# Tails on alternate partitions, a later load of q's first tail, and two batches' features dealt anew, in an attention kernel with a feed-forward layer

## The chip, the cores and the metric

One core of one Trainium2 chip. The metric is the device time of one launch in microseconds (us). A run that is over 1.5% above the fastest of its kernel is called slow, and ratios use the others, the fast ones.

## The reference

Eight batches of eight heads with 576 positions of 64 elements; linear attention with a cosine weight, then a feed-forward layer with a squared ReLU.

```python
def phi(x, c, s):                       # c, s: cos and sin of pi/2 * position / 576
    r = np.maximum(x, 0.0)
    return np.concatenate([r * c, r * s], axis=-1)
q_p, k_p = phi(q, cos_w, sin_w), phi(k, cos_w, sin_w)
kv  = np.einsum('bhsf,bhsd->bhfd', k_p, v)
z   = np.sum(k_p, axis=2)
num = np.einsum('bhsf,bhfd->bhsd', q_p, kv)
den = np.einsum('bhsf,bhf->bhs', q_p, z)[..., None] + 1e-06
x   = (num / den) ...                   # to (4608, 512): positions by heads*64
r   = np.maximum(x @ w_in, 0.0)         # 512 -> 2048
out = (r * r) @ w_out                   # 2048 -> 512
```

## The kernel before

A batch has 576 positions: four tiles of 128 ("main", 1 MB for each of q, k and v) and a tail of 64. The tails of the upper and the lower four heads share one tile: heads 0 to 3 on partitions 0 to 63, heads 4 to 7 on 64 to 127.

```python
def load(src, nm, b, eng):
    main = inp.tile([P, H, J, D], F32, name=nm, tag=nm, bufs=2)
    tail = inp.tile([P, HH, D], F32, name=nm + "t", tag=nm + "t", bufs=2)
    eng.dma_start(out=main[:, :, :, :], in_=...)
    for g in range(2):
        eng.dma_start(
            out=tail[g * TAIL : (g + 1) * TAIL, :, :],
            in_=src[b, g * HH : (g + 1) * HH, MAIN:S, :].rearrange("h p d -> p h d"),
        )
```

TensorE's work is a list of 144 slots (`gemm1` and `gemm2` of all batches). Attention's small pieces are hung on slots by hand: `k` are the slots in which k and v of a batch get their features, `f` those of q, `kv` the product, `d` the division. `qpT` is q's features transposed by DMA, `xT` the attention output transposed by DMA; both, and most loads, are issued by SP, in order. w_in, w_out and the loads of batches 1 to 3 are issued by GpSimd.

```python
at(14, load_batch, 3, nc.gpsimd, "qkv")
plan(2, k=(21, 22, 23, 24, 25), f=(18, 19, 20, 22, 23), kv=(26, 26), d=(27, 28, 29, 31, 33))
plan(3, k=(30, 32, 33, 34, 35), f=(27, 29, 31, 32, 33), kv=(36, 36), d=(37, 38, 39, 40, 41))
for b in range(4, B):
    at(second[b - 3] + 6, load_batch, b, nc.sync, "kv")     # slot 32 for batch 4
    at(first[b - 2] + 9, load_batch, b, nc.sync, "q")       # slot 43 for batch 4
    ...
```

One more tile matters for what follows, though the argument of the change does not mention it: a table of zeros for TensorE's warm-up, `zeros = const.tile([P, FP], BF16)`, 1024 bytes in each partition. It stands ahead of all weights and inputs in SBUF.

## Time and profile before

| | before |
|---|---|
| time, median of 4 runs | 293.31 us (292.41 to 293.62) |
| span of the profiled run | 291.0 us |
| TensorE (PE) busy | 281.0 us, 97% |
| PE idle 19 to 64 us | 0.20 us |
| PE idle 64 to 110 us | 1.17 + 0.61 + 1.31 us |
| PE idle 110 to 250 us | 0.09 + 0.29 us |

A windows view gives, for a stretch of the span, how long each engine was busy; the stretch less PE's busy time is PE's idle time. Columns: stretch, length, busy us of PE, PEld, DVE, ACT and POOL, the granted clock, the DMA engines' busy share, GB/s.

```profile
19.00:64.00 45.00, 44.80 (x491) 34.29 (x489) 29.95 (x72) 26.16 (x38) 19.66 (x28) 1.00 1.01 281
```

DMA is full here (share 1.01), and TensorE waits for nothing.

### The profile page before, as it was taken

To read this page: it belongs to the slowest core of one execution; us is meant where nothing else is said; L and a number is where in the kernel's file an instruction comes from. 1 tells how busy PE (TensorE), PEld (TensorE's weight loads), DVE (VectorE), ACT (ScalarE), POOL (GpSimd) and SP (SyncE) were. 2 spreads that over 40 slices of the span, in tenths; PEclk is the share of its full clock that TensorE was granted. 3 is DMA by queue.
4 is the path that set the end of the run, shared out by engine and by line. 5 is a ranking of instruction groups with operands and counts; after the bars stand their busy time and mean duration, and the time that the engine had idled before them with its cause. 6 is when DMAs were issued, how large, how long until landed. Compare 5 with 4: busy or idle time off the path is not lost.

```text
span 291.0 us, 7292 instructions
## 1 busy us (share of the span) xinstructions
PE 281.0 (97%) x3045; PEld 236.1 (81%) x3045; DVE 201.5 (69%) x450; ACT 164.7 (57%) x251; POOL 39.2 (13%) x67
## 2 busy tenths in 40 slices
PE   8999999998999989999999999999999999999994
PEld 3479855888677979898988888988998888889883
DVE  1467665596399487877588777977677877546584
ACT  3565752779748749655783358835695451265110
POOL 1552505750000000000002000000000000000011
PEclk9999999999999999999999999999999999999999
DMA  6999994999649996799519995399809540300014
GB/s 218 299 206 286 356 227 150 352 363 285 103 120 163 291 203 177 176 289 262 167 73 196 314 206 164 92 254 297 221 16 214 131 48 2 144 2 2 0 76 142
DMA packets 76641, 53.04 MB, mean 182 GB/s; under 512 B 52000, under 2 KB 71712, under 8 KB 76608
## 3 DMA queue, kind: packets, MB, share of 16 engines
q1 hardware_dynamic: 66816, 29.24, 43.7%
q0 software_dynamic: 9648, 23.20, 27.1%
q8 instruction: 24, 0.39, 0.5%
q10 hardware_dynamic: 144, 0.13, 0.1%
q14 instruction: 9, 0.07, 0.1%
HBM read 36.70 MB, written 9.44 MB: 159 GB/s over the span
## 4 chain that ended last, share of the span: by engine, by line
PE 83%; DVE 5%; DMA 4%; ACT 3%; SPq 2%; issue 1%; DVEq 0%
PE hps L383 40%; PE ya L525 9%; PE yc L525 8%; PE yu L525 7%; PE yv L525 5%; PE num L310 3%; DMA q<-in_q_dram 3%; PE kz L241 3%; PE yps L432 2%; PE yh L432 2%; PE yps L456 2%; DMA qpT<-qpt 2%; DVE ysb L537 2%; ACT rt L391 1%; PE tq L284 1%; SPq L69 1%
## 5 line engine op out<-in xcount | busy, mean ns | idle before, releaser
L383 PEld LDWEIGHTS <-w1sb 128*128 128x128 bf16 x1312 | 112.9, 98 | 13.6 <-issue 2.9
L383 PE MATMUL hps<-xT,w1sb 128*128 128x256 bf16 (+1 forms) x1056 | 119.0, 269 | 1.1 <-DVE ysb L537 0.6
L391 ACT ACTIVATE rt<-hps 128x1024 bf16<-128x1024 f32 x72 | 73.7, 1024 | 66.7 <-PE hps L383 43.3
L398 DVE TENSOR_TENSOR gT<-rt 128x1024 bf16<-128x1024 bf16 x64 | 43.9, 686 | 21.4 <-ACT rt L391 21.3
L525 PEld LDWEIGHTS <-gs 128*128 128x128 bf16 x480 | 46.9, 98 | 5.5
L525 PEld LDWEIGHTS <-gT 128*128 128x128 bf16 x312 | 29.8, 98 | 3.5
L410 POOL DMA_DIRECT2D out_dram<-ysb x14 | 7.7, 549 | 173.0 <-DVE ysb L537 145.6
L181 ACT ACTIVATE kp<-k,sin_col 128x512 bf16<-128x512 f32 x32 | 22.4, 718 | 3.1 <-DMA k<-in_k_dram 3.1
L324 DVE TENSOR_TENSOR x<-num,rden 128x512 bf16<-128x512 f32 x32 | 22.1, 691 | 1.1
L181 ACT ACTIVATE qp<-q,sin_col 128x512 bf16<-128x512 f32 x32 | 22.1, 722 | 1.2 <-DMA q<-in_q_dram 1.2
L320 DVE TENSOR_SCALAR den<-num 128x8 f32<-128x8 f32 (+1 forms) x40 | 6.5, 163 | 21.2 <-PE num L310 21.2
L521 DVE TENSOR_TENSOR gs<-gT 128x1024 bf16<-128x1024 bf16 x26 | 17.8, 683 | 0.0
L383 PE MATMUL hps<-xTt,w1sb 128*128 128x128 bf16 x256 | 15.1, 219 | 0.8 <-ACT rt L391 0.8
L171 DVE TENSOR_SCALAR qp<-q,cos_col 128x512 bf16<-128x512 f32 x32 | 14.7, 485 | 1.7 <-DMA q<-in_q_dram 1.7
L525 PE MATMUL yc<-w2sb,gs 128*128 128x256 bf16 x120 | 15.6, 273 | 0.0
L525 PE MATMUL ya<-w2t,gs 128*128 128x256 bf16 x120 | 15.6, 273 | 0.0
L525 PE MATMUL yu<-w2sb,gs 128*128 128x256 bf16 x120 | 15.6, 273 | 0.0
L525 PE MATMUL yu<-w2t,gs 128*128 128x256 bf16 x120 | 15.6, 273 | 0.0
L576 ACT COPY s<-yu 128x256 f32<-128x256 f32 x15 | 5.6, 373 | 16.6 <-PE yu L525 16.6
L200 ACT CAST vext<-v 128x512 bf16<-128x512 f32 x23 | 14.2, 615 | 1.3 <-DMA v<-in_v_dram 1.3
L525 PE MATMUL yc<-w2sb,gT 128*128 128x256 bf16 x104 | 13.5, 273 | 0.0
L525 PE MATMUL ya<-w2sb,gT 128*128 128x256 bf16 x104 | 13.5, 273 | 0.0
(93 smaller groups left out, 333.0 us busy)
## 6 DMA issues: line engine op xcount, KB each, us to landing
out_dram<-ysb POOLq DMA_DIRECT2D x14, 512.0 KB, 4.5
k<-in_k_dram SPq DMA_DIRECT2D x5, 1024.0 KB, 7.7
v<-in_v_dram SPq DMA_DIRECT2D x5, 1024.0 KB, 9.0
q<-in_q_dram SPq DMA_DIRECT2D x5, 1024.0 KB, 5.6
q<-in_q_dram POOLq DMA_DIRECT2D x3, 1024.0 KB, 12.4
k<-in_k_dram POOLq DMA_DIRECT2D x3, 1024.0 KB, 10.1
v<-in_v_dram POOLq DMA_DIRECT2D x3, 1024.0 KB, 8.8
w1sb<-in_moe_w_in_dram POOLq DMA_DIRECT2D x4, 512.0 KB, 8.6
```

The costliest lines, as they stand in the source:

```text
L171: nc.vector.tensor_scalar(out=dst[:, :, 0:D], in0=src, scalar1=0.0, scalar2=cos_col[:, j : j + 1], op0=ALU.max, op1=ALU.mult,)
L181: nc.scalar.activation(out=dst[:, :, D:F], in_=src, func=ACTF.Relu, scale=sin_col[:, j : j + 1])
L200: copy(out=vx[:, j, h0:h1, 0:D], in_=piece("v", b, j)[:, h0:h1, :])
L241: nc.tensor.matmul(out=kz[:, half, hh * E1 : (hh + 1) * E1], lhsT=lhsT, rhs=rhs, start=(j == 0 and hh == 0), stop=(j == J and hh == HH - 1),)
L310: nc.tensor.matmul(out=out, lhsT=lhsT, rhs=kvz[:, half * HH + hh, :], start=True, stop=True)
L324: nc.vector.tensor_tensor(out=x_of(b, j).rearrange("p (b k) (l d) -> p b k l d", b=n, l=2), in0=n4[:, :, :, 0:D].rearrange("p b (k l) d -> ...
L383: nc.tensor.matmul(out=out, lhsT=w1sb[:, kb, hb * P : (hb + 1) * P], rhs=rhs, start=(kb == 0), stop=(kb == KB - 1),)
L391: nc.scalar.activation(out=rt[:, :, :], in_=hps[:, :, :], func=ACTF.Relu)
L398: nc.vector.tensor_tensor(out=dst, in0=rt[:, :, :], in1=rt[:, :, :], op=ALU.mult)
L432: nc.tensor.matmul(out=ypss[b][tt], lhsT=gTs[b][:, hb, tt * P : (tt + 1) * P], rhs=w2sb[:, hb, :], start=(hb == 0), stop=(hb == HB - 1),)
L521: nc.vector.tensor_tensor(out=t[:, :, :], in0=in0, in1=in1, op=op)
L525: nc.tensor.matmul(out=acc, lhsT=lhs[:, hb, :], rhs=rhs[:, hb, :], start=(hb == 0), stop=(hb == HB2 - 1),)
```

## The change

The intent: let the tail loads reach all ports of SBUF and save four matmuls for each batch; get w_in 0.13 MB earlier; and move features of batches 2 and 3 between ScalarE and VectorE, so that the waits between 64 and 110 us go. The core of the diff:

```diff
-    def load(src, nm, b, eng):
-        main = inp.tile([P, H, J, D], F32, name=nm, tag=nm, bufs=2)
-        tail = inp.tile([P, HH, D], F32, name=nm + "t", tag=nm + "t", bufs=2)
 ...
+            kqv[nm, b] = inp.tile([P, NB * D], F32, name=nm, tag=nm, bufs=2)
 ...
+                out=tail_of(nm, b).rearrange("(p g) h d -> p g h d", g=2)[:, g],
 ...
-    zeros = const.tile([P, FP], BF16, name="zeros")
+    zeros = const.tile([P, P], BF16, name="zeros")
 ...
+    half_of = const.tile([P, 2], F32, name="half_of")
 ...
+            for g in range(2):
+                dst, half = vextts[b % 2][:, g, :, 0:D], half_of[:, g : g + 1]
+                if eng is nc.scalar:
+                    eng.activation(out=dst, in_=piece("v", b, j), func=ACTF.Copy, scale=half)
 ...
-            at(k[j], att_k, b, j, feat_cos_act if shared and j % 2 else feat_cos)
-            at(k[j], att_v, b, j, nc.scalar if shared and (b > 2 or j % 2) else nc.vector)
+            at(k[j], att_k, b, j, feat_cos_act if j in act_cos else feat_cos)
+            at(k[j], att_v, b, j, nc.scalar if j in act_v else nc.vector)
 ...
         d=(27, 28, 29, 31, 33),
+        act_cos=(),
+        act_v=(1,),
 ...
-        k=(30, 32, 33, 34, 35),
-        f=(27, 29, 31, 32, 33),
-        kv=(36, 36),
-        d=(37, 38, 39, 40, 41),
+        k=(27, 28, 30, 31, 32),
+        f=(33, 34, 35, 36, 36),
+        kv=(37, 37),
+        d=(38, 39, 40, 41, 42),
+        act_cos=(0, 1, 2, 3),
 ...
-        at(second[b - 3] + 6, load_batch, b, nc.sync, "kv")
+        at(36 if b == 4 else second[b - 3] + 6, load_batch, b, nc.sync, "kv")
 ...
-        load_batch(0, nc.sync, "kvq")
+        load_batch(0, nc.sync, "kv")
+        load_main("q", 0, nc.sync)
 ...
+        load_tail("q", 0, nc.gpsimd)
```

Main and tail now share one tile. With heads of both halves on alternate partitions, one matmul over all 128 partitions serves two heads: v's tail is copied twice, once with the odd and once with the even partitions set to zero (`half_of`). Batch 2 gives ScalarE's cosines and one v copy to VectorE; batch 3 has k first and q later, its cosines on ScalarE; the load of batch 4 moves from slot 32 to 36.

## The prediction

> **What bounds the kernel now.** I read the page first: the busy shares and the chain that ended last.
>
> ```profile
> PE 281.0 (97%) x3045; PEld 236.1 (81%) x3045; DVE 201.5 (69%) x450; ACT 164.7 (57%) x251; POOL 39.2 (13%) x67
> ...
> PE 83%; DVE 5%; DMA 4%; ACT 3%; SPq 2%; issue 1%; DVEq 0%
> ```
>
> TensorE is the bound: 281.0 of 291.0 us busy. The change removes almost no TensorE work, so it can win only the 10 us in which TensorE stands. The stretches (columns: span, then busy us of PE, PEld, DVE, ACT, POOL, the clock, DMA share, GB/s) say where those are:
>
> ```profile
> 0.00:19.00 19.00, 16.94 (x134) 8.48 (x135) 8.45 (x27) 10.14 (x18) 8.68 (x19) 1.00 0.97 247
> ...
> 64.00:78.00 14.00, 12.83 (x167) 10.70 (x166) 7.86 (x17) 13.34 (x20) 0.18 (x1) 1.00 1.04 239
> 78.00:96.00 18.00, 17.39 (x172) 13.53 (x171) 14.27 (x36) 12.17 (x21) 1.06 (x2) 1.00 0.65 142
> 96.00:110.00 14.00, 12.69 (x173) 11.23 (x170) 10.83 (x25) 7.72 (x12) 0.00 (x0) 1.00 1.10 228
> 110.00:130.00 20.00, 19.91 (x229) 17.80 (x227) 15.88 (x38) 13.97 (x25) 1.06 (x2) 1.00 0.80 212
> 130.00:250.00 120.00, 119.71 (x1335) 107.21 (x1334) 90.60 (x196) 68.81 (x105) 5.89 (x11) 1.00 0.67 168
> ```
>
> From 110 to 250 us only 0.4 us are idle: what is gained before 110 us reaches the end undiminished, and later batches can only lose. Between 64 and 110 us 1.17 + 0.61 + 1.31 = 3.1 us are idle; that is where batches 2 and 3 have their features. Before 19 us the matmuls are mostly warm-up, so "busy" there hides a wait for loads. The rest of the idle time, about 4 us, is the last additions and the last store, which the change leaves alone.
>
> The timeline names the three idle places. In 64 to 78 us ScalarE is busy 13.34 of 14 us:
>
> ```profile
> 71.02 1.01 ACT L391 ACTIVATE rt<-hps 128x1024 bf16<-128x1024 f32 x1
> 71.93 0.71 ACT L181 ACTIVATE kp<-k,sin_col 128x512 bf16<-128x512 f32 x1
> 72.06 0.69 DVE L398 TENSOR_TENSOR gT<-rt 128x1024 bf16<-128x1024 bf16 x1 [1.57 <-ACT rt L391]
> 72.08 1.95 PE L383 MATMUL hps<-xTt,w1sb 128*128 128x128 bf16 x32 [0.84 <-ACT rt L391]
> ...
> 77.05 0.30 PE L241 MATMUL kz<-vextt,kpt 64*128 64x65 bf16 x8 [0.33 <-ACT kpt L181]
> ```
>
> Features of batch 2 stand ahead of `rt` in ScalarE's queue, so the PSUM buffer comes free late (0.84 us), and the tail of k is late (0.33 us). At 90.59 us the next batch's first matmul waits 0.61 us for VectorE. The third place:
>
> ```profile
> 96.88 0.55 SPq L64 DMA_DIRECT2D v<-in_v_dram  x1
> 97.53 3.61 SPq L69 DMA_DIRECT2D vt<-in_v_dram  x2
> 101.23 2.07 SPq L342 DMA_TRANSPOSE xTt<-xt  x1
> 103.41 1.20 SPq L267 DMA_TRANSPOSE qpT<-qpt  x1
> 108.38 0.32 PE L310 MATMUL num<-kvz,qpT 128*64 128x65 bf16 x8 [1.31 <-DMA qpT<-qpt]
> ```
>
> The SP queue is in order. The loads of batch 4 (93.36 to 101.14 us) hold up the transpose of batch 3's q tail, and TensorE waits 1.31 us for it.
>
> **What the skill says.** (1) "SBUF — State Buffer", section "Door 1: The DMA port swizzle", says that partitions 0 to 63 reach only 8 of the 16 ports (196 against 328 GB/s at 1 MiB). This is what alternate partitions aim at. The trace agrees only in part: from 5.5 to 6 us, when 432 of 468 packets are the tail of k, the mean is 279 GB/s, against 314 GB/s for 1 KB packets from 2.5 to 5 us. Two tail halves in flight seem to use both groups of ports already. (2) "DMA: Bandwidth & Descriptors", section "Issuing engines are not separate DMA queues", says that loads from all queues interleave on the same 16 engines. So q's tail, moved to the GpSimd queue, is not carried for nothing; it only comes later. (3) "TensorE: Matmul & The Clock Gate", section "Back-to-back issue gap", makes time follow the moving columns, not the contraction rows. The trace agrees: eight 256-column matmuls are 0.87 us on the chain, 109 ns each.
>
> **The change part by part.**
>
> *Start.* The first real matmul is at 18.74 us and hangs on q, which lands at 13.6 us behind k, v and two tails in the same queue. Both tails together are 1024 packets over 16 engines, 64 each. At the 279 GB/s above, 0.26 MB take 0.94 us; at 314 GB/s 0.84 us; at best, estimated as a third less per packet, 0.6 us. So q lands 0.1 to 0.35 us earlier. q's own tail stood behind q, so taking it away gains q nothing; it frees 0.13 MB, about 0.4 us, for w_in, whose slices reach TensorE just in time. Against this: the v tail is now two VectorE operations (the old one 0.28 to 0.41 us, the new ones estimated at the 0.34 us of the k tail's, so +0.3 us) and the copy of kz is two (0.59 becomes 2 x 0.37, the 256-column copies' duration). kvz was ready at 13.02 us and its reader starts at 15.85 us, so both fit. I take **-0.3 us**.
>
> *Tail matmuls.* Eight of 65 columns at 30 ns (40 in 1.21 us) become four of 130 at 55 ns: 0.24 to 0.22 us per batch, **-0.1 us** in all. The tail of `num` now loads every second column as weights; I expect no cost.
>
> *Batch 2 re-dealt.* ScalarE loses two cos (0.62 us of pitch each) and one v copy (0.51), 1.75 us; VectorE gains 2 x 0.48 + 0.42 + 0.3 = 1.7 us and has 6.1 idle in 64 to 78. Walking ScalarE from `rt` at 67.74 with those pitches, the `rt` that freed the buffer at 72.04 is done at 71.3, and the k tail at 75.4, before its matmuls. TensorE's full 1.17 us come back, less 0.25 for the buffer freed at 71.3 instead of 71.05: **-0.9 us**.
>
> *Batch 3 re-dealt.* Its k moves ahead (slots 27 to 32, cos all on ScalarE), its q behind (33 to 36). VectorE loses 5 operations before 90 us, so the 0.61 us wait should fall to the 0.27 us seen at other batch ends: **-0.35 us**. ScalarE then has 4 x (0.62 + 0.61 + 0.51) + 0.41 + 0.8 + four copies, 10 us, in some 11.5: tight, but it fits. The k/v load of batch 4 moves from slot 32 to 36, behind the q tail transpose, which removes its wait: **-1.3 us**.
>
> Together 0.3 + 0.1 + 0.9 + 0.35 + 1.3 = 2.95 us less, if nothing replaces these waits.
>
> **Rivals.** *A: the later load of batch 4 is itself too late.* Slot 36 ends near 94 us in the changed kernel. ScalarE's `rt` and two q features follow, so the second transpose is issued near 95.8 and the load near 98 to 99, 5 us later than the old 93.36. Old: first transpose issue at 91.67, v landed at 106.4, 14.7 us later. New: 95.8 + 14 = about 109.5 to 110. Slot 42, whose first ScalarE work includes v, would be reached at 105, so v's copy wants its data at 107. From the first v copy (old 110.61) to the end of the v tail (116.81) are 6.2 us, plus 0.45 for the second masked copy. So the kz tail starts near 109.5 + 6.65 = 116.1 instead of 117.57. The net gain of all parts up to there is then 1.5 us, not 2.95: a DMA wait of some 1.5 us takes the place of those removed. Time about 291.8. For it: all issue times come from one in-order queue. Against it: the five-us shift is a walk, and every 1 us of error moves the result by 1.
>
> *B: the second masked v copy on ScalarE holds up every later batch.* Per batch +0.4 (v tail) +0.15 (kz copy). Between the old v tail's end and its matmuls are 0.76, 0.83 and 0.82 us in batches 4, 5 and 6, so it fits. If I am wrong by 0.5 us in four batches it costs 2 us: time 292 to 293.
>
> *C: nothing hides.* All waits go and the load is in time: 293.25 - 2.95 = 290.3; a start quicker by another 0.9 us through the ports makes 289.4.
>
> **Range and chances.** A at 291.8 gets 55%, C at 290.3 gets 35%, B at 292.7 gets 10%: the weighted mean is 291.4 us. The low end is C with the quicker start, the high end A with half of B's loss. Over 2% faster would be under 287.4 us and needs more than all the idle time before 270 us that I found, so 4%; over 2% slower needs a new wait of 9 us, so 1%.
>
> **What would show it.** `rt` no longer holds TensorE near 72 us, and the first batch-3 matmul waits 0.3 us or less. No wait for qpT near 107 us. q lands between 13.2 and 13.5 us and `hps` starts near 18.4. Near 105 to 117 us ScalarE waits 2 to 4 us for v of batch 4 (A) or not (C). From 120 to 250 us TensorE is idle under 0.5 us; if it is idle for more at every kz tail, B is right. Wrong would be: 256-byte packets much quicker with q landing before 13 us, or a wait for w_in, w_out or batch 1's loads between 20 and 45 us, since two more small loads stand ahead of them in the GpSimd queue.

## The result and the profile after

The changed kernel took **296.22 us** (median of 4 runs, 295.61 to 297.04) against 293.31 us. The ratio of the fast runs is 1.0106, with a 95% interval of 1.007 to 1.0142. Ratios here are the mean time of one kernel's fast runs over that of the other's of the same rounds, so not quite the ratio of the medians that are quoted. The change is slower by 1%, and outside the predicted range. The page of the changed kernel, its busy line and its chain by engine:

```profile
PE 281.4 (95%) x3008; PEld 236.0 (80%) x3013; DVE 203.5 (69%) x461; ACT 167.5 (57%) x263; POOL 39.8 (14%) x68
...
PE 70%; DMA 20%; DVE 5%; POOL 2%; issue 1%; SPq 1%; DVEq 0%; ACT 0%
```

PE's work is the same (281.4 us), but it stands for 13.4 us instead of 10.0, and the share of DMA in the chain that ended last rose from 4% to 20%. The windows view of the changed kernel tells where:

```profile
0.00:19.00 19.00, 16.44 (x120) 8.22 (x121) 8.41 (x33) 9.80 (x18) 7.83 (x18) 1.00 0.92 231
19.00:64.00 45.00, 43.73 (x474) 33.15 (x474) 29.34 (x70) 25.05 (x38) 17.66 (x25) 1.00 0.97 249
64.00:78.00 14.00, 13.72 (x179) 11.95 (x175) 11.12 (x26) 12.68 (x19) 3.64 (x6) 1.00 1.07 311
78.00:96.00 18.00, 17.37 (x166) 12.99 (x165) 13.10 (x32) 13.89 (x25) 1.06 (x2) 1.00 0.60 134
96.00:110.00 14.00, 13.84 (x180) 12.16 (x177) 10.66 (x24) 9.43 (x14) 0.00 (x0) 1.00 0.96 208
110.00:130.00 20.00, 16.22 (x182) 14.06 (x176) 13.54 (x33) 11.77 (x23) 1.06 (x2) 1.00 1.03 215
130.00:250.00 120.00, 119.67 (x1335) 107.29 (x1334) 91.14 (x199) 72.14 (x112) 5.36 (x10) 1.00 0.75 173
```

PE's idle time, before and after: 2.06 to 2.56 (0 to 19 us), 0.20 to 1.27, 1.17 to 0.28, 0.61 to 0.63, 1.31 to 0.16, 0.09 to **3.78** (110 to 130 us), 0.29 to 0.33. The re-deal did what it was to do at 64 to 78 and 96 to 110 us (2.0 us gained). Two new losses are larger: 3.7 us at 110 to 130 us and 1.1 us at 19 to 64 us.

The one at 19 to 64 us, from the chain that ended last (start, us, what):

```profile
30.89 10.95 DMA w2sb<-in_moe_w_out_dram
41.88 0.59 PE yh L497 x2
```

The second quarter of w_out needs 10.95 us from issue to landing, and the first product that reads this quarter waits for it, 0.91 us. The one after 110 us, from the timeline (start, us, engine, line, operation; in brackets the idle time before it and what ended it):

```profile
95.01 6.71 SPq L321 DMA_TRANSPOSE qpT<-qp  x2
...
105.34 0.47 SPq L84 DMA_DIRECT2D v<-in_v_dram  x1
...
112.93 0.62 ACT L244 CAST vext<-v 128x512 bf16<-128x512 f32 x1 [3.15 <-DMA v<-in_v_dram]
...
115.20 0.36 ACT L641 COPY s<-yu 128x256 f32<-128x256 f32 x1
115.22 0.53 SPq L84 DMA_DIRECT2D q<-in_q_dram  x1
115.61 1.03 PE L590 MATMUL yu<-w2sb,gs 128*128 128x256 bf16 x8 [1.91 <-ACT s L641]
...
121.16 1.33 ACT L220 ACTIVATE qp<-q,sin_col 128x512 bf16<-128x512 f32 x2 [1.26 <-DMA q<-in_q_dram]
...
122.52 5.86 SPq L321 DMA_TRANSPOSE qpT<-qp  x2
...
127.91 0.42 PE L364 MATMUL num<-kvz,qpT 128*128 128x65 bf16 x8 [1.44 <-DMA qpT<-qp]
```

Batch 4's v is loaded only behind batch 3's transposes and lands at 112.9 us. ScalarE stands 3.15 us before v's copy; the copy `s` that frees a PSUM buffer of the running product stands behind it in ScalarE's queue, so TensorE loses 1.91 us in a product that has nothing to do with batch 4. Then q of batch 4, issued behind further transposes at 115.22 us, is late as well and costs another 1.44 us. That is rival A of the prediction, but more than twice as large as it was worked out: 3.7 us more idle time, against 1.5.

### The profile page after: what moved, and what is told of

The parts are those of the page before. It is cut to its first block, busy times and chain, and to the rows that moved or that the text cites. A ratio compares the mean times of both kernels' runs of the same rounds, so it can differ in the third digit from the quotient of the medians.

```text
span 294.8 us, 7240 instructions
## 1 busy us (share of the span) xinstructions
PE 281.4 (95%) x3008; PEld 236.0 (80%) x3013; DVE 203.5 (69%) x461; ACT 167.5 (57%) x263; POOL 39.8 (14%) x68
## 4 chain that ended last, share of the span: by engine, by line
PE 70%; DMA 20%; DVE 5%; POOL 2%; issue 1%; SPq 1%; DVEq 0%; ACT 0%
PE hps L448 33%; PE yc L590 8%; PE ya L590 8%; DMA qpT<-qp 7%; PE yu L590 7%; DMA q<-in_q_dram 6%; PE yv L590 4%; DMA w2sb<-in_moe_w_out_dram 4%; PE num L364 3%; DMA v<-in_v_dram 3%; PE yh L497 2%; PE yps L497 2%; PE kz L284 2%; DVE ysb L602 1%; PE yps L521 1%; POOL w1sb L147 1%
## 5 line engine op out<-in xcount | busy, mean ns | idle before, releaser
L448 PEld LDWEIGHTS <-w1sb 128*128 128x128 bf16 x1312 | 112.9, 98 | 12.4 <-issue 1.7
L220 ACT ACTIVATE kp<-k,sin_col 128x512 bf16<-128x512 f32 (+1 forms) x40 | 26.2, 675 | 3.5 <-DMA k<-in_k_dram 3.5
L244 ACT CAST vext<-v 128x512 bf16<-128x512 f32 x22 | 13.5, 614 | 4.7 <-DMA v<-in_v_dram 4.7
L210 DVE TENSOR_SCALAR kp<-k,cos_col 128x512 bf16<-128x512 f32 (+1 forms) x28 | 12.0, 441 | 4.9 <-DMA k<-in_k_dram 4.9
L364 PEld LDWEIGHTS <-qpT 128*128 128x128 bf16 (+1 forms) x240 | 10.0, 100 | 5.8 <-DMA qpT<-qp 3.1
L364 PE MATMUL num<-kvz,qpT 128*128 128x65 bf16 (+1 forms) x240 | 11.7, 195 | 2.2 <-DMA qpT<-qp 2.0
```

What stands on the lines that cost most here:

```text
L210: nc.vector.tensor_scalar(out=dst[:, :, 0:D], in0=src, scalar1=0.0, scalar2=cos_col[:, c : c + 1], op0=ALU.max, op1=ALU.mult,)
L220: nc.scalar.activation(out=dst[:, :, D:F], in_=src, func=ACTF.Relu, scale=sin_col[:, c : c + 1])
L244: copy(out=vext_of(b, j)[:, h0:h1, 0:D], in_=piece("v", b, j)[:, h0:h1, :])
L364: nc.tensor.matmul(out=out, lhsT=lhsT, rhs=kvz[:, half * HH + hh, :], start=True, stop=True)
L448: nc.tensor.matmul(out=out, lhsT=w1sb[:, kb, hb * P : (hb + 1) * P], rhs=rhs, start=(kb == 0), stop=(kb == KB - 1),)
```

## The experiments

Each was run in five rounds against the kernel before on the same chip, after a profiled run. The ratios leave slow runs out: one run of six in e1, e2, e4, e8, e14 and e16, more where the text says so.

### First call: one part undone, or alone

**e1_load_at_32**: the changed kernel with batch 4's k and v at slot 32.

```diff
-        at(36 if b == 4 else second[b - 3] + 6, load_batch, b, nc.sync, "kv")
+        at(second[b - 3] + 6, load_batch, b, nc.sync, "kv")
```

> The changed kernel with one thing undone: k and v of batch 4 are loaded at slot 32 again, not 36. Theory L (the later load is the largest loss): of the 3.78 us in which TensorE stands between 110 and 130 us, under 0.6 are left; in exchange the transpose of batch 3's q tail stands behind the loads again, and 0.8 to 1.3 us of waiting for qpT come back between 96 and 110 us. Net about 2.4 us less: 293.8 us (293.0 to 294.6). Rival M (the masked v copies and slower transposes of the new layout make batch 4 late, not the slot): time stays within 1 us of 296.2 and at least 2 us of idle time stay between 110 and 130 us.

Measured: **302.25 us**, ratio 1.0298 (1.026 to 1.0335). Both theories missed. From the timeline:

```profile
97.97 7.76 SPq L321 DMA_TRANSPOSE qpT<-qp  x2
...
105.70 0.54 PE L364 MATMUL num<-kvz,qpT 128*128 128x65 bf16 x8 [5.22 <-DMA qpT<-qp]
106.05 3.47 PE L448 MATMUL hps<-xT,w1sb 128*128 128x256 bf16 x16
109.36 0.41 PE L364 MATMUL num<-kvz,qpT 128*128 128x65 bf16 x8
```

With the re-deal, q of batch 3 gets its features after k, so not only its tail but both of its large transposes stand behind the loads; TensorE waits 5.22 us. It then pays a second time: 16 matmuls of 256 columns take 3.47 us instead of the 1.91 us that they take elsewhere in this trace, at a granted clock of 0.88 for the stretch from 96 to 110 us. The Trainium skill ("TensorE: Matmul & The Clock Gate", section "HAM oscillation — how this bites in real kernels") warns of idle gaps over about 3.4 us; this trace agrees, with 5.22 us. (In e7, below, a wait of 1.92 us preceded the same fall.) So the later load is not an oversight of the change: the re-deal needs it.

**e2_qtail_first**: the changed kernel with q of batch 0 loaded whole by SP.

```diff
-        load_batch(0, nc.sync, "kv")
-        load_main("q", 0, nc.sync)
+        load_batch(0, nc.sync, "kvq")
 ...
-        load_tail("q", 0, nc.gpsimd)
```

> The changed kernel with q of batch 0 loaded whole on SP again, no load of its tail in the GpSimd queue. Theory Q (the two small loads push the first quarter of w_out behind further loads): the wait of the first yh for w2sb near 41 us disappears, TensorE idle between 19 and 64 us falls from 1.27 to 0.2 to 0.4 us, the first quarter of w_out is issued near 16.5 us again instead of 20.3; time about 295.2 us (294.8 to 295.6). Rival (the wait comes from slower packets in the run, whatever the order): the wait stays at 0.6 us or more and the time within 0.4 us of 296.2.

Measured: 296.46 us, ratio 1.0089 (1.0055 to 1.0123), like the changed kernel. The wait for w2sb fell only from 0.91 to 0.58 us. Theory Q falls for the most part: the order of the two small loads is not what makes w_out late.

**e3_deal_only**: the kernel before with the re-deal and the load at slot 36, nothing of the layout.

```diff
+        act_cos=(), act_v=(1,),                        # plan of batch 2
-        k=(30, 32, 33, 34, 35), f=(27, 29, 31, 32, 33), kv=(36, 36), d=(37, 38, 39, 40, 41),
+        k=(27, 28, 30, 31, 32), f=(33, 34, 35, 36, 36), kv=(37, 37), d=(38, 39, 40, 41, 42),
+        act_cos=(0, 1, 2, 3),                          # plan of batch 3
-        at(second[b - 3] + 6, load_batch, b, nc.sync, "kv")
+        at(36 if b == 4 else second[b - 3] + 6, load_batch, b, nc.sync, "kv")
```

> The kernel before with the re-deal of batches 2 and 3 and the load at slot 36 alone; tails on two halves, q loaded whole first. Theory L: the re-deal gains its 2.0 us before 110 us, the late load loses 3 to 3.7 us after it: 294.6 us (294.0 to 295.2), TensorE idle in 110 to 130 us 3 to 3.8 us. Rival M (layout makes batch 4 late): idle there under 1 us and a time of about 291.3 us.

Measured: 292.67 us, ratio 0.9988 (0.9943 to 1.0032): no loss and no proven gain. In the profiled run, its slowest, PE stood 2.93 us between 110 and 130 us. So the late load costs there as theory L says, though less than in the changed kernel (3.78 us), and the whole is 1.9 us under L's number. That points to something in the layout that is dear.

**e4_layout_only**: the changed kernel with everything undone but the layout: the edits of e1 and e2 together, and the diff of e3's two plans the other way round.

> The changed kernel with everything undone but the alternate partitions (with the masked v copies, the four tail matmuls, the merged buffers, the split copy of kz). Theory N (the layout itself does nothing): 293.3 us, within 0.4 of before; 256-byte packets take 18 ns; k, v and q land within 0.3 us of before. Rival P (ports): q lands 0.3 us or more earlier and the time is 292.8 or less. Rival S (the layout slows the DMA transposes and the start): qpT and xT pairs take 4.5 us or more in SP's queue as in the changed kernel, k lands at 6.8 us, and the time is 293.9 us or more.

Measured: 294.72 us, ratio 1.0049 (1.0018 to 1.0079). Neither N nor P; the time is rival S's, some 1.4 us more, though k landed at 6.33 us and not late as S had it. Its pairs of qpT in batches 5 to 7 took 4.56 to 5.55 us in SP's queue, as S has it, against 3.99 to 4.21 us before. Its 256-byte packets took 18 ns, as in the kernel before, and q landed at 14.16 us. In the first ten profiled runs q landed between 13.66 and 14.65 us, with the old layout (13.66 to 14.47) as with the new one, so the start differs from run to run and no gain of the layout is to be seen in it.

### Second call: what in the layout, and a better load

Reading the GpSimd queue of both kernels side by side showed one part of the cost. Before:

```profile
34.85 0.91 POOL L64 DMA_DIRECT2D q<-in_q_dram  x1
47.10 1.26 POOL L69 DMA_DIRECT2D qt<-in_q_dram  x2 [11.34 <-issue]
```

After:

```profile
48.93 0.90 POOL L84 DMA_DIRECT2D q<-in_q_dram  x1 [12.39 <-DVE qp L210]
```

This is q of batch 2. Its buffer was batch 0's. Before, the 1 MB main could be issued at 34.85 us and only the small tail waited for the last reader of batch 0's tail (slot 12). With main and tail in one tile, the whole megabyte waits: 48.93 us. All later loads of batches 2 and 3 move, and the first store behind them goes from 62.96 to 67.86 us.

**e5_own_buffers**: the changed kernel with tails in tiles of their own.

```diff
-            kqv[nm, b] = inp.tile([P, NB * D], F32, name=nm, tag=nm, bufs=2)
+            kqv[nm, b] = inp.tile([P, H, J, D], F32, name=nm, tag=nm, bufs=2)
+            kqv[nm + "t", b] = inp.tile([P, HH, D], F32, name=nm + "t", tag=nm + "t", bufs=2)
```

> The changed kernel with tails in tiles of their own again (the alternate partitions, masked copies and everything else kept). Theory G (one buffer for main and tail makes the 1 MB load of q of batch 2 wait for the last reader of q's tail of batch 0 at slot 12): that load is issued near 36.5 us instead of 48.93, the GpSimd queue is through with its loads about 4 us earlier (first stores near 63 to 64 us instead of 67.9), and the 0.58 us wait for qpT at 80 us goes; the loss at 110 to 130 us stays, since SP's order is the same: 295.2 us (294.6 to 295.8). Rival: the merging costs nothing because DMA is full later anyway: 295.9 to 296.5.

Measured: 295.26 us, ratio 1.0060 (1.0025 to 1.0094). As theory G has it: q of batch 2 was issued at 35.82 us, the wait for qpT at 80 us is gone and PE is not idle at all between 78 and 96 us. About 1 us of the loss is this by the medians; the intervals of the two ratios overlap, so the trace shows it better than the times.

**e6_layout_own_buffers**: e4 with the same edit.

> The layout alone (alternate partitions, masked copies, four tail matmuls) but with tails in tiles of their own. Theory G (the merging is the whole of the 1.2 us that the layout lost): 293.4 us (293.0 to 293.9), no wait over 0.3 us for qpT at 80 us, 110 to 130 us idle under 0.5 us. Rival S (alternate partitions or masked copies slow the transposes): pairs of qpT in batches 5 to 7 still take 4.5 us or more and the time stays at 294.3 or more.

Measured: 294.40 us, ratio 1.0034 (0.9999 to 1.0068): the waits for DMA are small (0.41 us at most), but about 1 us seems to be left; the interval just reaches 1. The time is rival S's; the cause that S names is tested below. One wait in its trace is for the layout's engine work: 0.50 us for vextt, v's masked tail, before the tail of kz in batch 3.

**e7_b4_by_gpsimd**: the kernel before, re-deal, k and v of batch 4 by GpSimd at slot 26; **e8_q3_later**: the same, q of batch 3 at slot 24.

```diff
-    at(14, load_batch, 3, nc.gpsimd, "qkv")
+    at(14, load_batch, 3, nc.gpsimd, "kv")            # e8 only
+    at(24, load_batch, 3, nc.gpsimd, "q")             # e8 only
 ...
-        at(second[b - 3] + 6, load_batch, b, nc.sync, "kv")
+        at(26 if b == 4 else second[b - 3] + 6, load_batch, b, nc.gpsimd if b == 4 else nc.sync, "kv")
```

> The kernel before with the re-deal, and k and v of batch 4 loaded by the GpSimd queue at slot 26 (where it is idle) instead of by SP at slot 36. Theory E (the load of batch 4 is the only thing the re-deal lost): v of batch 4 lands before 95 us, no transposes stand behind it, TensorE idle from 110 to 130 us under 0.5 us: 290.6 us (289.9 to 291.4). Rival C (the loads collide with the transposes of batch 2's x at 82 to 91 us): TensorE waits 1 us or more there and the time is 292 or more.

> As the run before, and q of batch 3 loaded at slot 24 instead of with k and v at slot 14: 1.1 MB less stand beside batch 2's transposes at 64 to 80 us. Theory: the second pair of qpT of batch 2 lands 2 to 3 us earlier, the wait for it at 80 us (0.6 to 1.4 us in the kernels with the re-deal) falls under 0.3, 0.5 to 1 us less than the run before: 290.0 us (289.3 to 290.9). Rival: q of batch 3 or k and v of batch 4 come late in exchange, and the time is no better than the run before.

Measured: their fast runs are good (ratios 0.9926 and 0.9916), but three of e7's six runs (296.65 to 305.8 us) and one of e8's (301.25 us) were slow. The ratios leave those out and flatter these kernels. What the slow runs spend their time on is shown under e13; why some runs fall into it and others not is left open.

### Third call: is it the alternate partitions?

The trace's DMA records have each packet's duration. In the six profiled kernels with the new layout, the 4096-byte packets with which GpSimd's loads arrive between 20 and 48 us took a median of 192 ns; in the four without it, 161 ns. These packets carry k, v and q. The obvious suspect was the alternate partitions.

**e11_dma_alternate**: the kernel before, tails written to alternate partitions and read as before. **e12_dma_halves**: e6 with tails written to halves. Their outputs are wrong, which doesn't matter for the times.

```diff
-                out=tail[g * TAIL : (g + 1) * TAIL, :, :],
+                out=tail[:, :, :].rearrange("(p g) h d -> p g h d", g=2)[:, g],     # e11; e12 the reverse
```

> The kernel before with one edit: the tails of k, v and q are written to alternate partitions, and everything reads them as before, so the result is wrong on purpose. Theory D (alternate partitions slow the loads themselves): the 4096-byte packets of the GpSimd queue take a median of 192 ns, as in all six profiled kernels with that layout, instead of 161 to 165 ns as in the four without; the first yh waits 0.2 us or more for w2sb near 41 us, and the time is 293.9 to 294.6 us. Rival M (the masked copies and the second kvz copy on ScalarE cost the 1 us): packets may be slower, but the time stays within 0.4 us of before.

> The other half of the same question: the layout kernel with tails in tiles of their own, all its engine work (masked copies, four tail matmuls, two kvz copies), but the tails loaded to halves as before; wrong on purpose. Theory D: 4096-byte packets at 161 to 165 ns again and a time of 293.3 us, within 0.4 of before. Rival M: the time stays at 294.3 us or more, as with alternate partitions.

Measured: e11 292.49 us, ratio 0.9990 (0.9955 to 1.0024), packets at 161 ns; e12 296.86 us, ratio 1.0121 (1.0094 to 1.0149), packets at 191 ns. Theory D falls on both sides: alternate partitions neither slow the packets nor cost time.

**e9_b4_at_29** and **e10_b4_split**: the load of batch 4 behind the store at 85 us, whole or k alone. Both also have the re-deal and q of batch 3 at slot 24 (the two lines marked "e8 only" above).

```diff
-        at(second[b - 3] + 6, load_batch, b, nc.sync, "kv")
+        if b == 4:
+            at(29, load_batch, b, nc.gpsimd, "k")     # e9: "kv" here, and no line below
+            at(36, load_batch, b, nc.sync, "v")
+        else:
+            at(second[b - 3] + 6, load_batch, b, nc.sync, "kv")
```

> Kernel before, re-deal, q of batch 3 at slot 24, k and v of batch 4 in the GpSimd queue at slot 29, behind the store at about 85 us, so that they cannot meet the transposes of batch 2's q at 74 to 82 us. Theory E: no run of the six over 294 us (the two kernels with the load at slot 26 had runs of 296.7 to 305.8), no wait over 1 us before 96 us; 290.5 us (289.7 to 291.5). Rival C: the loads now meet batch 2's second x transpose at 90 us, TensorE waits 1 us or more there and some runs are again over 296.

> As the run before, but only k of batch 4 goes by GpSimd at slot 29; v stays on SP behind batch 3's transposes at slot 36. Half the load, 3.5 us, fits between the two x transposes: v lands near 107 instead of 110 to 113 us, the wait for ScalarE's s near 115 us is under 0.5 us; 291.0 us (290.2 to 291.8), with no run over 294. Rival: v is still late, idle in 110 to 130 us over 1.5 us, and the time is 292 or more.

Measured: e9 296.10 us, ratio 1.0088 (1.0058 to 1.0118), all six runs fast: rival C, in every run. 2 MB in the GpSimd queue meet a transpose of SP:

```profile
101.39 3.51 PE L383 MATMUL hps<-xT,w1sb 128*128 128x256 bf16 x16 [3.39 <-DMA xT<-x]
104.74 0.41 PE L310 MATMUL num<-kvz,qpT 128*128 128x65 bf16 x8
104.99 1.91 PE L383 MATMUL hps<-xT,w1sb 128*128 128x256 bf16 x16
```

After the wait of 3.39 us the same 16 matmuls take 3.51 us, and 1.91 us again two lines on: the lower clock of e1 once more.

e10: **291.35 us** (290.41 to 292.3), ratio 0.9937 (0.9912 to 0.9961). The expectation held. The windows view of e10:

```profile
96.00:110.00 14.00, 13.83 (x183) 12.04 (x181) 11.05 (x27) 9.60 (x15) 0.00 (x0) 1.00 0.76 170
110.00:130.00 20.00, 19.91 (x239) 17.61 (x237) 16.50 (x39) 12.12 (x21) 1.09 (x2) 1.00 0.86 245
```

PE stands 0.09 us between 110 and 130 us. Only v is left behind the transposes: it is issued at 99.92 us, and ScalarE does not wait for it. Against e3, two loads have moved, k of batch 4 and q of batch 3; what each is worth was not run.

### Fourth and fifth call: where the buffers start

What all kernels with slow packets share is the address of their buffers. The compiled programs tell it: before, k, v and q start at multiples of 512 bytes in a partition (k at 62976). The changed constants (zeros 768 bytes shorter, new small tiles) move w_in, w_out, k, v and q down by 640 bytes: k starts at 62336, which is 384 modulo 512 and 128 modulo 256. (What lies behind them moves by other amounts: x, xT and qpT are at 128 modulo 256 before and at 0 after.)

Not every packet is slower. w_in and w_out arrive in packets of 1024 bytes, with a median of 98 ns from 20 to 48 us in both kernels, and SP loads k, v and q into the same buffers in packets of 1024 bytes, with a median of 46 ns in both.

**e13_changed_aligned**: the changed kernel, zeros 128 bytes longer. **e14_before_shifted**: the kernel before, zeros 384 bytes longer.

```diff
-    zeros = const.tile([P, P], BF16, name="zeros")
+    zeros = const.tile([P, P + 64], BF16, name="zeros")       # e13
-    zeros = const.tile([P, FP], BF16, name="zeros")
+    zeros = const.tile([P, FP + 192], BF16, name="zeros")     # e14
```

> The changed kernel with one edit: the table of zeros is 128 bytes longer in each partition, so that k, v and q start at 0 modulo 512 bytes as in the kernel before, not at 384; qp at 256 not 128. Theory H (the start of the buffers): 4096-byte packets of the GpSimd queue at a median of 161 to 165 ns instead of 192, pairs of qpT in batches 5 to 7 under 4.4 us instead of 4.5 to 5.5, and 1 to 2 us less: 294.8 us (294.0 to 295.4). Rival M (the masked copies and split kvz copy on ScalarE): packets and time as in the changed kernel, 295.8 to 296.7 us.

> The kernel before with one edit: the table of zeros is 384 bytes longer, so that k, v and q start at 384 modulo 512 bytes and qp at 128, as in the changed kernel. Theory H: 4096-byte packets at 192 ns, pairs of qpT in batches 5 to 7 at 4.5 us or more, w2sb waited for near 41 us, and 294.3 us (293.8 to 295.2). Rival M: nothing changes, 293.3 within 0.4.

Measured: the packets follow the address both ways: 165 ns in e13, 187 ns in e14. The times cannot be used. e13 had runs from 291.87 to 303.7 us, all but one of them slow, so that no ratio is given. e14 had 295.16 to 301.73 us, ratio 1.0144 (1.0097 to 1.0192): slower, but with a spread like that of e7.

The profiled runs of e7, e8, e13 and e14 are slow ones, and show where the time goes. First the kernel before, then e13:

```profile
63.85 9.69 SPq L267 DMA_TRANSPOSE qpT<-qp  x2
```

```profile
63.90 21.24 SPq L321 DMA_TRANSPOSE qpT<-qp  x2
...
85.29 0.62 PE L364 MATMUL num<-kvz,qpT 128*128 128x65 bf16 x8 [7.17 <-DMA qpT<-qp]
```

Batch 2's pair of qpT holds SP's queue for 21.24 us, TensorE waits 7.17 us for it, and the granted clock is 0.50 from 83.4 to 90.2 us. In e7, e8 and e14 the longest waits for a transpose between 78 and 96 us are 1.92, 4.47 and 3.21 us, and a stretch of 3.3 us or more at a clock of 0.50 begins in or soon after each. So in these four runs the time goes to late transposes and a lower clock with them; what makes the transposes late in some runs is not shown.

**e15_aligned_own_deal**: e13 with tails in tiles of their own (e5's edit) and q loaded whole first (e2's edit).

> The changed kernel with its buffers at 0 modulo 512 bytes, tails in tiles of their own and q loaded whole first; left of the change are alternate partitions, masked copies, four tail matmuls, the re-deal and the load at slot 36. Theory H with G: that is the re-deal alone plus nothing: 292.9 us (292.2 to 293.8), as e3. Rival M: the engine work of the layout still costs 1 us, 294 or more.

Measured: 293.25 us, ratio 0.9993 (0.9959 to 1.0027); no slow run, packets at 161 ns. This kernel has all of the layout's engine work (masked copies, split copy of kz) and is as fast as the re-deal alone (e3, 0.9988), within intervals of some 0.4%. Rival M, at 294 us or more, falls; a wait of 0.33 us for vextt at batch 4's kz tail is what is left of it in the trace.

**e16_layout_best**: e15 with the loads of e10, but for q of batch 3.

> As the run before, with k of batch 4 in the GpSimd queue at slot 29 and v on SP at slot 36, as in e10 (q of batch 3 stays at slot 14). If the layout is neutral, as e10: 291.4 us (290.7 to 292.2), idle in 110 to 130 us under 0.5 us. If its engine work on ScalarE costs something where batch 4 is tight: 292.3 us or more and a wait for vextt at batch 4's kz tail.

Measured: 292.53 us, ratio 0.9964 (0.9926 to 1.0001). PE stands 1.41 us between 110 and 130 us, 1.19 of it for batch 4's qpT. The time is that of the expectation's second half, but the wait for vextt that it names is not there. No gain of the layout over e10 is seen; since q of batch 3 differs too, a loss is not shown either.

**e17_own_and_aligned**: e5 with zeros 128 bytes longer, the same edit as e13. **e18_split_old_deal**: the kernel before with the loads of e10 and its own deal of features.

> e5 (the changed kernel with tails in tiles of their own, 295.26 us) with one edit: the table of zeros 128 bytes longer, so that k, v and q start at 0 modulo 512 bytes. Theory H (the start of the buffers costs 2 us): packets at 161 to 165 ns, the wait for w2sb at 41 us (1.24 us in e5) under 0.3, and 293.3 us (292.6 to 294.0). Rival (the load of q's tail behind w_in, which e15 had undone as well, costs part of it): the wait for w2sb stays over 0.6 us and the time is 294.2 or more.

> The kernel before with its own deal of features, and only the loads moved as in e10: q of batch 3 at slot 24, k of batch 4 by GpSimd at slot 29, v on SP at slot 36. If the moved loads alone remove the 1.3 us wait for batch 3's q tail and the re-deal is worth 1.2 to 1.5 us of its own (0.84 and 0.61 us of waiting for ScalarE and VectorE stay): 292.2 us (291.6 to 292.9). Rival: the re-deal is worth nothing beside the loads: 291.4, as e10.

Measured: e17 292.93 us (292.03 to 293.41), ratio 0.9969 (0.9937 to 1.0001), against 1.0060 for e5; the intervals do not overlap. **128 bytes in a table of zeros are worth 0.9%, 2.3 us between the medians.** Packets took 165 ns. The wait for w_out in e5 was

```profile
41.60 0.59 PE L495 MATMUL yh<-w2sb,gT 128*128 128x512 bf16 x2 [1.24 <-DMA w2sb<-in_moe_w_out_dram]
```

and e17 has none, though q's tail still stands behind w_in. Its windows view:

```profile
19.00:64.00 45.00, 44.64 (x486) 34.41 (x487) 30.54 (x74) 26.26 (x39) 21.26 (x30) 1.00 1.01 288
64.00:78.00 14.00, 13.66 (x167) 11.24 (x167) 9.44 (x21) 11.67 (x18) 0.00 (x0) 1.00 0.91 231
78.00:96.00 18.00, 18.00 (x180) 14.47 (x179) 15.00 (x36) 15.48 (x27) 1.06 (x2) 1.00 0.47 122
96.00:110.00 14.00, 13.84 (x180) 12.14 (x179) 11.15 (x28) 7.13 (x12) 0.00 (x0) 1.00 1.03 226
110.00:130.00 20.00, 16.96 (x192) 14.59 (x190) 13.47 (x33) 13.62 (x25) 1.06 (x2) 1.00 0.99 221
```

DMA moves 288 GB/s from 19 to 64 us, as before the change (281); the changed kernel moved 249. From 64 to 110 us PE stands 0.34 + 0.00 + 0.16 us: the whole gain of the re-deal. From 110 to 130 us it stands 3.04 us: the late load of batch 4, by itself. (In e5 it was 3.91 us, so the start of the buffers costs there too.)

e18: 292.40 us, ratio 0.9948 (0.9913 to 0.9982). The moved loads alone make most of e10's gain. Its trace still has the 0.84 us and 0.61 us waits that the re-deal takes away, but the ratios of e10 and e18 do not tell the two apart.

## Why the prediction was wrong

- **The re-deal** (batch 2: -0.9; batch 3: -0.35 and -1.3): right. Batch 2 gave 0.89 us (0.83 in e17). For batch 3 the wait before slot 34 went altogether in e17 (-0.61), though in the changed kernel a new wait for qpT at 80 us hid it; the wait for the q tail's transpose gave 1.15 us.
- **Rival A** (load of batch 4 itself too late, -1.5 us): the mechanism was right, the size was off. v lands at 109.94 us in e17, where the walk said 109.5 to 110. The term that was mis-sized is what the delay does afterwards: 2.95 us more idle time in 110 to 130 us (3.04 against 0.09) instead of 1.5. The walk counted only the path from v to the kz tail, and as far as that its sum is near: in e17 PE waits 1.38 us for `s`, which stands behind v's copies in ScalarE's queue, and 0.34 us at the kz tail. It left out that q of batch 4, behind later transposes in SP's queue, is late too (1.14 us).
- **The start** (-0.3): not there. 256-byte packets took 18 ns in both layouts, and q's landing varies by 1 us between runs.
- **Tail matmuls** (-0.1): not there. From the start of the group in batch 4 to the start of the next matmul are 0.23 us with eight (117.57 to 117.80) and with four (119.70 to 119.93).
- **Rival B** (masked copies hold up every batch): wrong. PE stands 0.33 us from 130 to 250 us, against 0.29. Only batch 4, whose v is late, waits for vextt (0.33 us in the changed kernel), and e15 shows no cost of the engine work in the time.
- **The list of what would be wrong** named a wait for w_out between 20 and 45 us and laid it to two small loads. The wait came; the reason was another (e2, e17).
- **The step that failed** is the one that took a cost only from operations that the diff adds, removes or moves. Two costs come from no operation. One is the start of the buffers: e5 to e17, 0.91% or about 2.7 us by the ratios, 2.3 us by the medians. The other is the merged tile: the changed kernel to e5, 0.46% or 1.3 us by the ratios, 1.0 us by the medians. These runs come from different rounds, e5 and e17 from different chips. Without the re-deal both look smaller: the merging moved the ratio by only 0.15% (e4 to e6), and e6, with shifted buffers, is only 0.34% over the kernel before. So the sizes, that of the merging above all, are less certain than that the costs are there. The sum from the kernel before: 293.3 - 0.83 - 0.61 - 1.15 (re-deal, as e17 shows it) + 2.95 (late load) + 2.3 + 1.0 = 297.0 us, against 296.2 measured. The same sum without the last two terms gives 293.7 us for e17, which took 292.93; those 0.7 us are unexplained, and of the size of the differences between rounds.

The Trainium skill has a mechanism that fits the first: "DMA: Bandwidth & Descriptors", section "How a descriptor splits into AXI transactions", says that "An AXI transaction can read less than 256 B, but it must start from a 256B-aligned address." A row of 64 fp32 elements is 256 bytes; at 128 modulo 256 it would straddle a boundary. The page speaks of reads, and what is shifted here is the destination; the packets of 1024 bytes, shifted alike, show nothing; and only 0 and 384 modulo 512 were tried, so the runs do not tell 256 from 512. The mechanism is therefore argued, and not well supported. What is shown is that the start of the buffers, and no engine work, takes the 4096-byte packets from 161 to 192 ns.

What stays open: why kernels e7, e8 and e13, and perhaps e14, have runs 5 to 15 us above their fastest; why packets of 256 and of 1024 bytes show nothing of the shift; and why, at shifted addresses, tails on halves (e12, ratio 1.0121) are dearer than on alternate partitions (e6, 1.0034), while at aligned ones they are alike (e11).

## What to carry to other kernels

After a change, compare the addresses of all DMA buffers, not only the instructions: a shorter constant table moved the buffers of k, v and q off a multiple of 512 bytes, and that cost about what the re-deal gained. Merging two small tiles into one also merges their waits: the early megabyte then waits for the last reader of the late kilobytes. And when a load is moved behind something to free a queue, follow its data to the end: whatever stands behind its consumers in an in-order queue is late with it, and splitting the load (e10, 291.35 us, the best kernel without a slow run) can serve both sides.

## What the Trainium skill lacked or had wrong

- "DMA: Bandwidth & Descriptors", section "How a descriptor splits into AXI transactions": it has the 256-byte rule for reads, with no time and no word on the destination. Here a destination at 384 instead of 0 modulo 512 bytes took 4096-byte packets of GpSimd's loads from 161 to 192 ns (19%), and the kernel from 292.93 to 295.26 us (e17 and e5), while packets of 1024 bytes stayed at 46 and 98 ns.
- "SBUF — State Buffer", section "Operand start alignment", says of its own runs that they timed nothing. The same numbers belong there.
- "SBUF — State Buffer", section "Door 1: The DMA port swizzle": it has no word on alternate partitions. Here two halves loaded by two DMAs in flight gained nothing from them (e11: ratio 0.9990, 18 ns for each 256-byte packet in both).
- "DMA: Bandwidth & Descriptors", section "Issuing engines are not separate DMA queues", says that DMAs interleave. It lacks what a transpose loses by that: with k and v in the other queue (e9) TensorE waited 3.39 us for a transpose in the profiled run, and all six runs were 294.6 us or more; with k alone (e10) it did not wait.
